# Score products of the first batch from three to two per group, with tail keys beside the local ones, and a new written order of all queues

## The chip, the cores and the metric

One core of a Trainium2 chip runs the whole kernel. The metric is the device time of one launch in microseconds (us). TensorE is called PE, VectorE DVE, ScalarE ACT, GpSimd POOL, and the queue of the sync engine, which issues nearly every DMA, SP.

## What is computed

Attention of 4 batches x 8 heads x 768 queries with head size 64, in which each query sees the keys closer than 16 to it and a summary (maximum) of every block of 32 keys; the values are v and the block means of v. The result, 3072 x 512, goes through a two-layer perceptron (512 to 2048 to 512) with GELU. All in float32 on the host side; the weights come as float64.

```python
k_sum = k.reshape(B, H, nb, block, D).max(axis=3)
v_sum = v.reshape(B, H, nb, block, D).mean(axis=3)
scores_l = scale * np.matmul(q, k.transpose(0, 1, 3, 2))
mask_l = np.abs(pos[:, None] - pos[None, :]) < window
scores_s = scale * np.einsum('bhsd,bhnd->bhsn', q, k_sum) + np.log(block)
a = softmax(np.concatenate([np.where(mask_l, scores_l, -1e9), scores_s], axis=-1))
x = np.matmul(a, np.concatenate([v, v_sum], axis=2))      # heads joined: 3072 x 512
h = x @ w_in;  g = 0.5 * h * (1.0 + erf(h * inv_sqrt2));  out = g @ w_out
```

## The kernel before

**Tiling.** Attention runs in 24 units: unit u is one batch, four heads and 256 queries, that is four query tiles of 64. Units 0 to 5 are the first batch. For a tile, 128 slots hold the keys a query may see: before the change 64 local keys in slots 0 to 63, 24 block summaries in 64 to 87 (`SLOT_SUM`), eight masked slots, and 32 tail keys in 96 to 127 (`SLOT_TAIL`). A unit has eight groups of 128 slots, four for each half of the array rows (`e`); in one group two tiles (`c`) sit in the two halves of the output partitions.

**Steps of a unit.** Units 0 to 5 are `wide`: `f_mask` (L721) lays the mask into PSUM with float16 products, and `scores_wide` (L760) adds float32 products straight from `kp0` (keys of the first batch, tail and local keys contiguous) and `ks32` (summaries). A float32 product stands as two records on PE, each with a weight load of its own. Later units split q and k into two float16 parts and multiply 48 times. Then `maximum_p` (DVE), `exponent_p` (ACT), `recip` (DVE), and a normalisation on ACT (`s_norm`) or DVE (`p_norm`). Units 0 to 2 turn the probabilities on PE (`p_turn`, kept by ACT in `p_keep`); later ones by DMA: `s_p_hi` (ACT), `p_lo` (DVE), two `turn` steps (L890, SP). `values` (L915) multiplies by v, which `load_v` brings, `s_load_vs` completes with the block means (`sum_vt`, `mean_vt`), and, from unit 3 on, `v_hi` (ACT) and `v_lo` (DVE) split. `take_hi` (ACT) and `take_lo` (DVE) take the result out of PSUM as two float16 parts of x.

**Perceptron.** Two units make one chunk of 256 tokens. `phase1h` (half of the contraction, L980) and `phase1` (L967) multiply by w_in for chunks 0 to 3, later pairs of chunks go through seven half-size `product` steps (L1004); `gelu`, `g_hi`, `g_lo` follow; `phase2` (L1073) and, for the last two pairs, `s_product`/`s_last` multiply by w_out. Weights arrive as float64 in `stage`, `gh` and `gl`, are turned to float32 by three DVE steps each (`wh_bits`, `wi_bits`, `wo_bits`) and split by `wi_hi`/`wo_hi` (ACT) and `wi_lo`/`wo_lo` (DVE). `warm` steps are products of ones whose result nobody reads.

**Order.** Nothing reorders at run time or by a planner at build time: the string `ORDER` (L74) lists 1648 steps, each is issued when its turn comes, and so every engine's queue is the sequence of its own steps in that string. The five PSUM banks (`bank`), the two `stage` halves and other rings are handed out in the same order. Around the change PE's queue begins: `warm 2`, `warm 3`, `f_mask 0`, `scores 0`, `warm 0`, `f_mask 1`, `scores 1`, `warm 1`, `f_mask 2`, `scores 2`, `p_turn 0 0`, `p_turn 0 1`, `sum_vt 0`, `p_turn 1 1`, `f_mask 3`, `scores 3`, `p_turn 1 0`, `values 0`, `sum_vt 1`, `p_turn 2 0`, `p_turn 2 1`, `f_mask 4`, `scores 4`, `values 1`, then ten `phase1h 0` steps with `values 2`, `f_mask 5`, `values 3` and `scores 5` among them, then `phase1 1 1`.

Of the kernel before, what the change touches and what calls it, by code (L numbers as in the profile page):

```python
# [1340 lines left out]
```

## Time and profile before

| what | value |
|---|---|
| median of 3 runs | 555.44 us (555.1 to 556.59) |
| the profiled execution | 556.61 us, span 554.8 us |
| PE busy | 544.9 us (98%) |
| DVE busy | 453.2 us (82%) |
| ACT busy | 425.3 us (77%) |
| DMA | 74.94 MB, mean 135 GB/s, 300 to 400 GB/s in the first 40 us |

The span runs from the first to the last instruction; the rest of the execution's time lies around it. An engine's share is a mean over stages that differ: DVE is at 82% in all, but a window of 20 us tells whether it has room there. "PEclk" is the clock that TensorE was granted, as a share of full speed. "issue" is idle time for which the profile shows no releasing event.

### The profile page before, as it was taken

How to read it: one execution, taken by the hardware profiler on the slowest of the kernel's cores; microseconds unless marked ns; L12 is line 12 of the kernel's file. 1: busy time of each engine (PE TensorE's matmuls, PEld its weight loads, DVE VectorE, ACT ScalarE, POOL GpSimd, SP SyncE). 2: the span in 40 equal slices, each digit the busy share in tenths (PEclk: the TensorE clock that was granted, in tenths of full speed). 3: DMA queues.
4: the chain of work that ended last, by engine and by line, in shares of the span. 5: the costliest groups of instructions: out<-in, count | busy, mean ns of one | idle time of the engine just before them, and what ended most of it. 6: DMA issues, size and time to landing. Idle time of an engine off the chain costs nothing.

```text
span 554.8 us, 14751 instructions
## 1 busy us (share of the span) xinstructions
PE 544.9 (98%) x6241; PEld 402.8 (73%) x6241; DVE 453.2 (82%) x638; ACT 425.3 (77%) x1005; POOL 0.8 (0%) x9
## 2 busy tenths in 40 slices
PE   8799999999999999999999999999999999999997
PEld 4678885457858665678665767756776888888886
DVE  4979999979989997989888674798799999885611
ACT  3978985759999998999999999997886585653320
POOL 0000000000000000000000000000000000000000
PEclk9989999999999999999999999999999999999999
DMA  8986585696879675554636461531440000100012
...
DMA packets 73635, 74.94 MB, mean 135 GB/s; under 512 B 46944, under 2 KB 52960, under 8 KB 73568
## 3 DMA queue, kind: packets, MB, share of 16 engines
...
q8 instruction: 49, 0.80, 0.6%
q14 instruction: 18, 0.15, 0.1%
...
## 4 chain that ended last, share of the span: by engine, by line
PE 94%; DMA 3%; DVE 1%; issue 1%; ACT 0%; SPq 0%; ACTq 0%; DVEq 0%
PE bank L1017 25%; PE bank L1080 10%; PE bank L1081 10%; PE bank L1082 10%; PE bank L1194 9%; PE ps_v L923 4%; PE bank L976 4%; PE bank L989 4%; PE bank L978 4%; PE bank L977 4%; PE ps_s L793 3%; PE ps_s L1194 2%; PE ps_v L1194 2%; PE ps_s L775 1%; DMA q<-in_qd_dram 1%; PE bank L876 1%
## 5 line engine op out<-in xcount | busy, mean ns | idle before, releaser
L1080 PE MATMUL bank<-w_out_h,gh 128*128 128x512 f16 x256 | 97.1, 379 | 0.0
L1081 PE MATMUL bank<-w_out_l,gh 128*128 128x512 f16 x256 | 97.0, 379 | 0.0
L1082 PE MATMUL bank<-w_out_h,gl 128*128 128x512 f16 x256 | 97.0, 379 | 0.0
L1017 PEld LDWEIGHTS <-w 128*128 128x128 f16 x640 | 62.0, 98 | 9.3
L1017 PEld LDWEIGHTS <-w_in 128*128 128x128 f16 x576 | 55.9, 98 | 8.6
L833 ACT ACTIVATE s<-s,s_top 128x128 f32<-128x128 f32 x144 | 55.8, 394 | 0.1
L1067 DVE SCALAR_TENSOR_TENSOR gl<-g,gh 128x512 f16<-128x512 f32 x76 | 51.0, 683 | 4.0 <-ACT gh L1063 3.9
L1063 ACT ACTIVATE gh<-g 128x512 f16<-128x512 f32 x76 | 46.6, 626 | 3.4 <-PE bank L1081 2.8
L1082 PEld LDWEIGHTS <-gl 128*128 128x128 f16 x256 | 25.1, 98 | 30.2
L1017 PE MATMUL bank<-x,w_in 128*128 128x256 f16 x384 | 46.6, 273 | 0.0
L1029 DVE TENSOR_TENSOR g<-bank,late 128x512 f32<-128x512 f32 x48 | 32.9, 686 | 14.3 <-PE bank L1017 13.8
L1080 PEld LDWEIGHTS <-gh 128*128 128x128 f16 x256 | 25.0, 98 | 26.7
L1081 PEld LDWEIGHTS <-gh 128*128 128x128 f16 x256 | 25.1, 98 | 26.0
L1017 PE MATMUL bank<-stage,w 128*128 128x256 f16 x320 | 44.0, 273 | 0.0
L1023 ACT ACTIVATE late<-bank 128x512 f32<-128x512 f32 x48 | 28.0, 591 | 20.6 <-PE bank L1017 19.9
L1017 PE MATMUL bank<-x,w 128*128 128x256 f16 x320 | 43.6, 273 | 0.0
L978 PE MATMUL bank<-x,w_in 128*128 128x256 f16 x144 | 39.3, 273 | 0.0
L976 PE MATMUL bank<-x,w_in 128*128 128x256 f16 x144 | 39.3, 273 | 0.0
L977 PE MATMUL bank<-x,w_in 128*128 128x256 f16 x144 | 39.2, 273 | 0.0
L1049 ACT ACTIVATE g<-bank 128x512 f32<-128x512 f32 x48 | 28.0, 589 | 9.2 <-PE bank L978 4.8
L1049 ACT ACTIVATE g<-g 128x512 f32<-128x512 f32 x48 | 29.2, 624 | 5.3 <-DVE g L1029 5.0
L870 ACT ACTIVATE s<-s,s_rec 128x128 f32<-128x128 f32 x104 | 31.8, 391 | 0.4 <-DVE s_rec L848 0.4
...
## 6 DMA issues: line engine op xcount, KB each, us to landing
...
```

The source lines that it names most:

```text
L833: nc.scalar.activation(self.s32[:, gs], score[:, ss], AF.Exp, bias=self.top[:, g : g + 1], scale=scale, accum_out=self.den[:, g : g + 1],)
L976: nc.tensor.matmul(dst, wh, xh, start=(k == 0), stop=False)
L977: nc.tensor.matmul(dst, wh, xl, start=False, stop=False)
L978: nc.tensor.matmul(dst, wl, xh, start=False, stop=(k == NCC - 1))
L1017: nc.tensor.matmul(dst, l, r[:, k], start=(first and e == 0 and k == 0 and n == 0), stop=(k == KH - 1 and n == 2), skip_group_check=True,)
L1049: nc.scalar.activation(g, h, AF.Gelu, scale=1.0 / (SC_X * SC_WI))
L1063: nc.scalar.activation(gh, two(g_slot(c, i)), AF.Copy, scale=SC_G)
L1067: nc.vector.scalar_tensor_tensor(out=gl, in0=two(g_slot(c, i)), scalar=SC_G, in1=gh, op0=ALU.mult, op1=ALU.subtract)
L1080: nc.tensor.matmul(t, gh[:, f, js], w_out_h[:, f, :], start=(n == 0), stop=False)
L1081: nc.tensor.matmul(t, gh[:, f, js], w_out_l[:, f, :], start=False, stop=False)
L1082: nc.tensor.matmul(t, gl[:, f, js], w_out_h[:, f, :], start=False, stop=(n == NFC - 1))
L1194: nc.tensor.matmul(acc[:, t * NH : (t + 1) * NH], a[:, f, js], b[:, f], start=(first and j == 0 and t == 0 and f == 0 and n == 0), stop=(f ...
```

## The change

Two things change together. First, for batch 0 the slots are laid out as 64 local keys, 32 tail keys, 24 summaries, eight masked ones. Local and tail keys are contiguous in `kp0`, so `scores_wide` makes one product of 96 columns and one of 24 for each tile instead of three of 64, 24 and 32: 32 float32 products per unit instead of 48, over the same 120 columns. The mask, the summary rows of `sum_vt`, `mean_vt`, `load_vs`, and the host layout of v follow; the number and size of their instructions stay, but for the 96 + 24 instead of 64 + 24 output rows of `sum_vt`. Second, `ORDER` is replaced: it holds the same 1648 steps with the same arguments in another sequence, on all queues. Of the order the part up to about 80 us is shown, old and new.

```diff
@@ -27,6 +27,7 @@
 KW = TQ + BLOCK
 SLOT_SUM = TQ
 SLOT_TAIL = TQ + BLOCK
+WIDE_TAIL, WIDE_SUM = TQ, TQ + BLOCK
@@ ORDER @@
-fetch_k 0 0, load_m16, load_q 0, fetch_k 0 1, fetch_wh 1 1, load_q 1, fetch_w_in 4, warm 2 9, warm 3 3, f_mask 0,
-prep_k 0 0, scores 0, maximum_p 0, prep_k 0 1, warm 0 12, f_mask 1, scores 1, exponent_p 0, fetch_wh 6 1, load_eye,
-load_q 2, warm 1 1, f_mask 2, scores 2, fetch_vt 0, fetch_wh 1 0, load_ind, load_q 3, fetch_wh 6 0, fetch_vt 1,
-load_v 0, fetch_w_in 2, wh_bits 1 1 0, wh_bits 1 1 1, wh_bits 1 1 2, recip 0, wi_hi 1 1, s_norm 0, fetch_w_in 0,
-load_v 1, load_q 4, p_turn 0 0, p_turn 0 1, sum_vt 0, wi_bits 4 0, maximum_p 1, wi_bits 4 1, exponent_p 1,
-wi_lo 1 1, wi_bits 4 2, maximum_p 2, wh_bits 6 1 0, wi_hi 4 1, exponent_p 2, wi_hi 4 0, p_keep 0 1, mean_vt 0,
-recip 1, wh_bits 1 0 0, p_norm 1, wh_bits 6 1 1, wh_bits 1 0 1, wh_bits 6 1 2, wi_lo 4 1, wh_bits 6 0 0,
-wh_bits 1 0 2, recip 2, wi_lo 4 0, wh_bits 6 0 1, p_keep 0 0, s_load_vs 0, p_turn 1 1, f_mask 3, scores 3,
-p_turn 1 0, values 0, fetch_wh 7 1, load_v 2, s_norm 2, maximum_p 3, wi_bits 2 0, take_hi 0, sum_vt 1, p_turn 2 0,
-p_turn 2 1, exponent_p 3, p_keep 1 1, mean_vt 1, p_keep 1 0, wh_bits 6 0 2, wi_bits 2 1, take_lo 0, f_mask 4,
-scores 4, s_load_vs 1, values 1, phase1h 0 4 0, wi_bits 0 0, wi_bits 2 2, wi_bits 0 1, wi_hi 1 0, recip 3,
-wi_bits 0 2, wi_hi 6 0, wi_hi 2 0, wi_hi 0 0, p_keep 2 1, take_hi 1, s_load_vs 2, p_keep 2 0, wi_hi 6 1,
-wh_bits 7 1 0, wi_lo 1 0, p_norm 3, wi_lo 6 0, wi_lo 0 0, take_lo 1, maximum_p 4, phase1h 0 1 0, phase1h 0 6 0,
-s_p_hi 3, wi_hi 2 1, exponent_p 4, values 2, wi_hi 0 1, take_hi 2, fetch_w_out 4, fetch_wh 7 0, fetch_w_in 3,
-load_v 3, load_q 5, turn 3 0, s_load_vs 3, v_hi 3, wi_lo 6 1, wi_lo 2 0, wh_bits 7 0 0, wh_bits 7 1 1, wo_bits 4 0,
-p_lo 3, wh_bits 7 0 1, turn 3 1, wh_bits 7 1 2, wh_bits 7 0 2, wi_lo 2 1, wi_lo 0 1, take_lo 2, v_lo 3, wi_bits 3 0,
-wo_bits 4 1, recip 4, wo_bits 4 2, phase1h 0 0 0, phase1h 0 6 1, phase1h 0 4 1, f_mask 5, phase1h 0 1 1,
-phase1h 0 2 0, phase1h 0 2 1, values 3, gelu 0 4, gelu 0 1, take_hi 3, g_hi 0 4, g_hi 0 1, take_lo 3, fetch_w_in 5,
-phase1h 0 0 1, scores 5, load_v 4, s_norm 4, wo_hi 4, wi_hi 7 0, s_load_vs 4, gelu 0 0, g_hi 0 0, gelu 0 2,
-wi_bits 3 1, wi_bits 5 0, g_lo 0 1, g_lo 0 4, wi_bits 5 1, wo_lo 4, phase1 1 1, phase1 1 4, phase1 1 6,
-fetch_w_out 0, wi_bits 5 2, wo_bits 0 0, wi_bits 3 2, wi_hi 5 1, v_hi 4, wi_lo 5 1, wo_bits 0 1, wi_hi 3 0,
-wi_hi 5 0, gelu 0 6, gelu 1 1, g_hi 0 6, wi_lo 5 0, wo_bits 0 2, wi_lo 7 0, v_lo 4, fetch_w_out 1, wo_hi 0,
-g_hi 1 1, g_lo 1 1, g_lo 0 0, wo_lo 0, phase1 1 2, gelu 1 4, g_hi 1 4, phase1 1 0, phase1h 0 5 0, phase1h 0 5 1,
-phase1 1 5, wi_hi 7 1, s_p_hi 4, wi_hi 3 1, fetch_w_out 7, load_q 7, load_v 5, wi_lo 3 0, gelu 1 0, g_hi 0 2,
-gelu 0 5, wo_bits 1 0, g_lo 1 4, wo_bits 1 1, wi_lo 3 1, wo_bits 1 2, gelu 1 5, wo_hi 1, g_hi 1 0, wi_lo 7 1,
...
+fetch_k 0 0, load_m16, load_q 0, fetch_k 0 1, load_eye, load_q 1, fetch_wh 6 1, fetch_wh 1 1, warm 2 9, warm 3 3,
+f_mask 0, prep_k 0 0, scores 0, maximum_p 0, prep_k 0 1, warm 0 12, f_mask 1, scores 1, load_q 2, fetch_wh 6 0,
+fetch_wh 1 0, fetch_vt 0, load_ind, fetch_w_in 4, load_q 3, load_v 0, fetch_vt 1, fetch_w_in 0, wh_bits 6 1 0,
+wh_bits 6 1 1, wh_bits 6 1 2, exponent_p 0, wi_hi 6 1, fetch_w_in 2, load_v 1, recip 0, s_norm 0, wh_bits 1 1 0,
+wh_bits 1 1 1, wh_bits 6 0 0, wh_bits 1 1 2, maximum_p 1, wh_bits 6 0 1, wi_hi 1 1, exponent_p 1, wi_lo 1 1,
+wh_bits 6 0 2, wh_bits 1 0 0, warm 1 1, f_mask 2, scores 2, maximum_p 2, p_turn 0 1, p_turn 0 0, sum_vt 0,
+wi_hi 6 0, exponent_p 2, p_keep 0 1, mean_vt 0, p_keep 0 0, s_load_vs 0, recip 1, wh_bits 1 0 1, p_norm 1,
+wi_lo 6 0, wi_bits 4 0, wh_bits 1 0 2, wi_hi 1 0, wi_lo 6 1, wi_bits 4 1, recip 2, wi_bits 4 2, s_norm 2,
+p_turn 1 0, p_turn 1 1, f_mask 3, scores 3, values 0, p_keep 1 1, p_keep 1 0, take_hi 0, maximum_p 3, wi_lo 1 0,
+sum_vt 1, p_turn 2 1, p_turn 2 0, mean_vt 1, exponent_p 3, s_load_vs 1, wi_bits 0 0, wi_bits 0 1, take_lo 0,
+wi_bits 0 2, phase1h 0 6 0, phase1h 0 1 0, f_mask 4, values 1, wi_bits 2 0, wi_bits 2 1, load_q 4, fetch_wh 7 1,
+recip 3, wi_hi 4 1, wi_hi 4 0, wi_hi 0 0, wi_bits 2 2, wi_hi 2 0, take_hi 1, wh_bits 7 1 0, scores 4, load_q 5,
+load_v 2, fetch_wh 7 0, fetch_w_in 3, fetch_w_out 4, p_keep 2 1, p_keep 2 0, s_load_vs 2, wi_hi 2 1, wi_lo 4 0,
+wh_bits 7 1 1, take_lo 1, phase1h 0 4 0, wi_lo 4 1, wi_lo 2 0, p_norm 3, phase1h 0 6 1, values 2, load_v 3,
+s_p_hi 3, turn 3 0, wi_lo 0 0, maximum_p 4, wi_lo 2 1, wh_bits 7 0 0, wi_bits 3 0, wh_bits 7 0 1, p_lo 3, take_hi 2,
+wi_hi 0 1, wi_lo 0 1, wh_bits 7 0 2, wh_bits 7 1 2, turn 3 1, exponent_p 4, wo_bits 4 0, take_lo 2, s_load_vs 3,
+v_hi 3, v_lo 3, phase1h 0 4 1, phase1h 0 2 0, phase1h 0 2 1, phase1h 0 0 0, phase1h 0 1 1, f_mask 5, scores 5,
+values 3, phase1h 0 0 1, wo_bits 4 1, gelu 0 6, wi_hi 7 1, wi_lo 7 1, wi_hi 7 0, take_hi 3, take_lo 3, wo_bits 4 2,
+wi_bits 3 1, gelu 0 0, gelu 0 4, wo_hi 4, recip 4, fetch_w_in 5, fetch_kx 3 3, load_q 6, fetch_w_out 0, load_v 4,
+wi_bits 5 0, wi_bits 3 2, wi_bits 5 1, wo_lo 4, s_norm 4, g_hi 0 0, s_p_hi 4, gelu 0 1, g_hi 0 4, g_hi 0 1,
+g_lo 0 0, wi_bits 5 2, wi_hi 5 1, wi_hi 3 1, gelu 0 2, wo_bits 0 0, g_lo 0 4, wi_lo 7 0, wo_bits 0 1, wi_lo 5 1,
+fetch_w_out 1, wo_bits 0 2, phase1 1 1, phase1 1 6, phase1 1 0, phase1 1 4, gelu 1 0, gelu 1 4, g_hi 1 0,
+s_load_vs 4, wi_hi 5 0, g_lo 1 0, p_lo 4, wi_lo 5 0, wo_hi 0, gelu 1 1, v_hi 4, wo_lo 0, v_lo 4, wi_hi 3 0,
+wo_bits 1 0, g_hi 1 1, g_hi 1 4, g_lo 0 1, wi_lo 3 1, g_lo 1 4, wo_bits 1 1, wi_lo 3 0, g_hi 0 2, wo_bits 1 2,
+phase1 1 7, phase1h 0 7 0, phase1h 0 7 1, phase1 1 5, phase1h 0 5 0, turn 4 0, turn 4 1, gelu 1 7, gelu 1 5,
+g_hi 0 6, wo_hi 1, load_v 5, s_load_vs 5, g_hi 1 5, load_q 7, fetch_w_out 7, load_mask, fetch_w_out 5, maximum_p 5,
+wo_lo 1, g_lo 0 6, wo_bits 7 0, g_lo 1 1, wo_bits 7 1, wo_bits 7 2, values 4, phase1 1 2, phase1h 0 3 0,
...
@@ -594,12 +595,12 @@
         total = bank.use(f"vt{h}", 2)
         for j in range(NTT):
             nc.tensor.matmul(
-                total[: SLOT_SUM + NBLK, :VH], ind_sb[:, P - SLOT_SUM + j * NBLK : P + (j + 1) * NBLK], vt0[:, h, j],
+                total[: WIDE_SUM + NBLK, :VH], ind_sb[:, P - WIDE_SUM + j * NBLK : P + (j + 1) * NBLK], vt0[:, h, j],
                 start=(j == 0), stop=(j == NTT - 1),
             )
 
     def mean_vt(h):
-        rows = slice(SLOT_SUM, SLOT_SUM + NBLK)
+        rows = slice(WIDE_SUM, WIDE_SUM + NBLK)
         nc.scalar.activation(
             vm0[rows, h * VH : (h + 1) * VH], bank.use(f"vt{h}", 2)[rows, :VH], AF.Copy, scale=1.0 / BLOCK
         )
@@ -690,7 +691,7 @@
 
         def load_vs(self, scalar=False):
             if self.b == 0:
-                rows = slice(SLOT_SUM, SLOT_SUM + NBLK)
+                rows = slice(WIDE_SUM, WIDE_SUM + NBLK)
                 means = vm0[rows, self.h0 * D : (self.h0 + UH) * D].rearrange("p (r e d) -> p r e d", r=NR, d=D)
                 means = means.unsqueeze(1).broadcast_to([NBLK, CT, NR, 2, D])
                 dst = self.v32[rows].rearrange("p (t r e) d -> p t r e d", t=CT, e=2)
@@ -733,7 +734,7 @@
                     cs = slice(c * TQ, (c + 1) * TQ)
                     dst = pse[e][cs].rearrange("p (n j) -> p n j", j=P)
                     nc.tensor.matmul(
-                        dst[:, :, SLOT_SUM : SLOT_SUM + NBLK], two[:, cs],
+                        dst[:, :, WIDE_SUM : WIDE_SUM + NBLK], two[:, cs],
                         logb.unsqueeze(1).broadcast_to([2, NG // 2, NBLK]), start=False, stop=False, skip_group_check=True,
                     )
 
@@ -762,20 +763,19 @@
             pse = [self.ps(e) for e in range(2)]
             for g in range(NG // 2):
                 r, t2 = g // 2, g % 2
-                for part in range(3):
+                for part in range(2):
                     for e in range(2):
                         for c in range(2):
                             rows, t = slice(e * D, (e + 1) * D), 2 * t2 + c
                             at, kb = g * P, c0 + t * TQ
                             at, k = (
-                                (at, kp0[rows, r0 + r, kb : kb + TQ]),
-                                (at + SLOT_SUM, ks32[rows, r0 + r]),
-                                (at + SLOT_TAIL, kp0[rows, r0 + r, kb + TQ : kb + TQ + P - SLOT_TAIL]),
+                                (at, kp0[rows, r0 + r, kb : kb + WIDE_SUM]),
+                                (at + WIDE_SUM, ks32[rows, r0 + r]),
                             )[part]
                             nc.tensor.matmul(
                                 pse[e][c * TQ : (c + 1) * TQ, at : at + k.shape[1]],
                                 self.q32[rows, (r * CT + t) * TQ : (r * CT + t + 1) * TQ], k,
-                                start=False, stop=(g == NG // 2 - 1 and part == 2),
+                                start=False, stop=(g == NG // 2 - 1 and part == 1),
                             )
 
         def scores(self):
@@ -1262,7 +1262,8 @@
 
 
 def _mask16():
-    m = _mask()[:, : (CT + 2) * TQ]
+    m = _mask()[:, : (CT + 2) * TQ].reshape(P, -1, P)
+    m = np.concatenate([m[:, :, :SLOT_SUM], m[:, :, SLOT_TAIL:], m[:, :, SLOT_SUM:SLOT_TAIL]], axis=2).reshape(P, -1)
     two, logb = np.zeros((P, P)), np.zeros((P, NBLK))
     two[:2] = 1.0
     logb[0] = np.float16(LOGB)
@@ -1289,7 +1290,8 @@
         for t in range(CT):
             r = (t0 + t) * TQ
             vw[u, :TQ, t] = vp[b, r : r + TQ, hs]
-            vw[u, SLOT_TAIL:, t] = vp[b, r + TQ : r + TQ + BLOCK, hs]
+            tail = SLOT_TAIL if b else WIDE_TAIL
+            vw[u, tail : tail + BLOCK, t] = vp[b, r + TQ : r + TQ + BLOCK, hs]
     qd, kd, vw = (a.reshape(nu, a.shape[1], -1) for a in (qd, kd, vw))
     kp = np.ascontiguousarray(k.transpose(0, 1, 3, 2).reshape(B, H // 2, P, S))
     kp[B - 1] = kp[B - 1].transpose(1, 0, 2).reshape(H // 2, P, S)
```

## Rows read from the trace of the kernel before

**Rows 1.** The profile page: span, and busy time, share and instructions by engine.
```profile
span 554.8 us, 14751 instructions
PE 544.9 (98%) x6241; PEld 402.8 (73%) x6241; DVE 453.2 (82%) x638; ACT 425.3 (77%) x1005; POOL 0.8 (0%) x9
```

**Rows 2.** Windows: length, busy PE, PEld, DVE, ACT, POOL; PEclk, DMA share, GB/s.
```profile
20.00:40.00 20.00, 17.48 (x319) 14.40 (x321) 17.11 (x32) 15.79 (x53) 0.00 (x0) 0.91 0.94 364
40.00:60.00 20.00, 19.96 (x339) 16.74 (x333) 19.83 (x30) 18.30 (x44) 0.00 (x0) 1.00 0.73 228
...
340.00:360.00 20.00, 19.55 (x236) 15.02 (x235) 14.42 (x21) 19.97 (x42) 0.00 (x0) 1.00 0.45 99
```

**Rows 3.** Chain of work that ended last, by time: start us, us, what.
```profile
17.98 1.65 PE bank L876 x13
19.62 0.72 issue
20.34 0.60 PE bank L876 x3
20.95 2.59 PE bank L596 x12
23.54 0.89 PE bank L876 x8
24.43 0.55 PE ps_s L730 x4
24.98 0.20 PE ps_s L735 x4
25.18 1.53 PE ps_s L775 x96
26.71 2.18 issue
28.89 1.67 PE bank L876 x8
...
58.31 0.22 PE bank L976
...
71.73 2.62 PE bank L989 x24
...
347.33 6.28 DMA pt<-p_l
```

**Rows 4.** DMA queues of the page: packets, MB, share of 16 engines.
```profile
q8 instruction: 49, 0.80, 0.6%
```

**Rows 5.** Timeline of PE in `scores 3`: start us, us, line, tile, shape, count.
```profile
25.27 0.26 PE L775 MATMUL ps_s<-misc,q 64*64 64x24 f32 x8
25.36 0.44 PE L775 MATMUL ps_s<-w_out_l,q 64*64 64x32 f32 x16
25.62 0.26 PE L775 MATMUL ps_s<-misc,q 64*64 64x24 f32 x8
```

**Rows 6.** Timeline of DVE from 10 to 36 us: `prep_k 0 1`, then pairs of neighbours.
```profile
10.02 1.75 DVE L555 TENSOR_REDUCE misc<-w_out_l 128x48 f32<-128x1536 f32 x1
...
23.17 0.68 DVE L406 SCALAR_TENSOR_TENSOR w<-gl,w 128x512 int32<-128x512 int32 x1
23.77 0.68 DVE L410 SCALAR_TENSOR_TENSOR w<-stage,w 128x512 int32<-128x512 int32 x1
...
34.35 1.22 DVE L410 SCALAR_TENSOR_TENSOR w<-gh,w 128x1024 int32<-128x1024 int32 x1
35.48 1.22 DVE L406 SCALAR_TENSOR_TENSOR w<-gh,w 128x1024 int32<-128x1024 int32 x1
```

**Rows 7.** Timeline of SP: the second `turn` of unit 3.
```profile
48.56 1.31 SPq L892 DMA_TRANSPOSE pt<-p_l  x1
```

**Rows 8.** Timeline of PE: after the stall in `scores 1`; and `values 3`.
```profile
14.29 0.18 PE L775 MATMUL bank<-misc,q 64*64 64x24 f32 x1 [0.94 <-issue]
...
54.42 0.95 PE L923 MATMUL ps_v<-pt,v_hl 128*64 128x64 f16 x48
```

More of the change, by code (lines that the diff above doesn't have):

```diff
@@ L115 @@
-g_hi 2 1, gelu 2 0, p_lo 6, load_q 10, load_k 10, turn 6 1, put 0 1, scores 8, phase1 2 2, phase1 2 6, t_add 1 0,
-recip 7, prep_k 2 0, v_hi 6, s_q_hi 9, gelu 2 4, gelu 2 2, g_hi 2 4, g_hi 2 0, s_k_hi 9, g_hi 2 2, v_lo 6, g_lo 2 1,
-load_v 7, fetch_v 3 0, values 6, phase1 2 3, add_mask 8, q_lo 9, p_norm 7, k_lo 9, gelu 2 6, g_hi 2 6, store 1 0,
-s_q_hi 10, take_hi 6, s_p_hi 7, s_k_hi 10, g_lo 2 0, q_lo 10, maximum 8, g_lo 2 6, take_lo 6, scores 9, phase1 2 5,
-phase1 2 7, phase2 1 7, k_lo 10, p_lo 7, g_lo 2 4, add_mask 9, exponent 8, recip 8, t_add 1 1, load_vs 7, load_k 11,
@@ L120 @@
-turn 7 1, turn 7 0, load_k 12, load_q 11, gelu 2 5, g_hi 2 5, v_hi 7, prep_v 3 0, prep_k_end 2 0, v_lo 7, load_v 8,
-fetch_k 2 1, put 1 0, load_vs 8, load_q 12, gelu 2 3, g_hi 2 3, store 1 1, s_norm 8, gelu 2 7, g_hi 2 7, phase2 2 0,
-phase2 2 1, values 7, t_add 1 2, t_add 1 3, g_lo 2 5, t_add 0 0, phase2 2 4, maximum 9, take_hi 7, s_p_hi 8,
-s_k_hi 11, s_q_hi 11, take_lo 7, g_lo 2 2, t_add 0 1, k_lo 11, t_add 2 1, q_lo 11, phase1 3 1, phase1 3 0,
-exponent 9, v_hi 8, prep_k 2 1, p_lo 8, turn 8 0, g_lo 2 3, recip 9, prep_k_end 2 1, p_norm 9, scores 10,
@@ new lines @@
+k_lo 8, maximum 7, exponent 7, phase1 2 0, phase1 2 4, scores 8, phase1 2 5, phase2 1 7, load_k 9, load_q 10,
+gelu 2 4, gelu 2 0, gelu 2 5, g_hi 2 5, s_q_hi 10, s_k_hi 9, g_hi 2 4, fetch_k 2 0, turn 6 0, prep_v 1 1, load_vs 6,
+put 0 1, load_q 11, load_k 10, p_lo 6, add_mask 8, recip 7, t_add 1 0, maximum 8, prep_k 2 0, t_add 0 1, phase1 2 1,
+phase1 2 3, v_hi 6, store 1 1, gelu 2 1, s_k_hi 10, gelu 2 3, g_hi 2 1, k_lo 9, scores 9, s_q_hi 11, turn 6 1,
+v_lo 6, p_norm 7, g_lo 2 5, prep_k_end 2 0, g_lo 2 1, values 6, g_hi 2 0, take_hi 6, s_p_hi 7, g_hi 2 3, exponent 8,
@@ new lines @@
+fetch_v 3 0, load_v 7, fetch_v 3 1, load_k 11, put 1 1, load_vs 7, turn 7 0, phase1 2 7, phase1 2 6, gelu 2 6,
+g_lo 2 0, take_lo 6, phase2 2 1, phase1 2 2, prep_v 3 0, q_lo 10, g_lo 2 3, phase2 2 0, t_add 1 1, p_lo 7,
+add_mask 9, g_lo 2 4, turn 7 1, k_lo 10, t_add 2 1, recip 8, s_k_hi 11, v_hi 7, v_lo 7, k_lo 11, gelu 2 7,
+store 1 0, s_norm 8, values 7, take_hi 7, scores 10, gelu 2 2, s_p_hi 8, phase2 2 5, take_lo 7, maximum 9,
+load_q 12, load_v 8, put 0 0, prep_v 3 1, q_lo 11, t_add 1 2, p_lo 8, exponent 9, s_q_hi 12, q_lo 12, recip 9,
@@ new lines @@
+v_lo 10, product 2 0 1, phase2 3 1, values 10, scores 13, s_q_hi 14, t_hi 0 0, s_p_hi 11, p_lo 11, t_hi 0 1,
+g_hi 3 6, gelu 3 7, maximum 12, exponent 12, keep 2 0 0, sx_hi 2 1, t_lo 0 0, product 2 1 1, phase2 2 7, g_lo 3 5,
+phase2 3 0, phase2 3 3, load_v 11, turn 11 0, load_vs 11, store 2 1, v_hi 11, g_hi 3 7, t_lo 0 1, t_hi 1 0,
+x_take 10, turn 11 1, load_q 15, g_lo 3 4, add_mask 13, phase2 3 5, t_add 3 0, put 2 0, k_lo 14, load_k 16, q_lo 14,
+maximum 13, sx_lo 2 1, product 2 0 2, exponent 13, v_lo 11, g_lo 3 7, t_add 3 1, values 11, scores 14, g_lo 3 6,
```

267 lines of the change are left out of this document (130 added, 137 removed).

## The prediction

> **What bounds the kernel now.** I read the page first: PE is busy for 544.9 of 554.8 us [rows 1], so no edit on another engine helps unless PE idles for it, and only 9.9 us of idle time exist. The windows then say where: PE idles 2.52 us between 20 and 40, 0.04 between 40 and 60 and 0.45 between 340 and 360 [rows 2]; the other windows up to 540 are full, and what remains lies in the first 20 us and behind the last product. So PE is the bound from about 29 us to the end, and its start is the only place with something to win. There the chain names two stalls that wait for nothing the profile shows, 0.72 us inside `p_turn 0` and 2.18 us after `scores 3` [rows 3]; a third, 0.94 us, stands in `scores 1` [rows 8]. DVE is the second engine to look at: it is busy for 19.83 of 20 us between 40 and 60 and idles only 2.89 between 20 and 40 [rows 2]. Whoever starts PE earlier must ask whether DVE can follow.
>
> **The stalls.** Between the second and the third stall PE takes 3 + 12 + 8 + 4 + 4 + 96 = 127 records [rows 3], each with its weight load: 254 instructions, 256 with two waits. The page counts 2 x 6241 PE instructions [rows 1], and one instruction queue moved 49 packets, 0.80 MB in all [rows 4]: 16 KB and about 255 instructions each. So PE's instructions come in pages of 256, and each of these stalls is a late page. One page is asked for, I take it, when the one before is entered: the page entered at 20.34 was followed by one at 28.89, 8.55 us later, and the one entered at 14.29 by the one at 20.34, 6.05 us later [rows 3, 8]. The Trainium skill, "Runtime: NRT & Kernel Launch", section "Instruction fetch mechanics", gives the same 256 instructions in 16 KiB blocks, fetched while the current block runs, and calls the crossing mostly hidden. By that rule these stalls would be nothing; the trace disagrees with its 0.94, 0.72 and 2.18 us while the DMA share is 0.94.
>
> **Part 1, the products.** A float32 product of 24 columns and its three partners occupy 25.27 to 25.36, 0.09 us; one of 32 and one of 64 together 0.26 [rows 5]; four such groups make the 1.53 us of a unit [rows 3]. The new product of 96 columns has no row. I bound it by the 0.26 of the two that it replaces and by the 0.16 that is left for 64 columns if 32 take 0.10, a little more than 24. A straight line through 32 and 64 columns gives 0.22; the floor is a cost per instruction alone. I take 0.20, nearer to the line: 0.06 saved in a group, 0.24 in a unit, with bounds of 0 and 0.4. Six units: 1.4 us (0 to 2.4). In units 0 to 2 PE waits anyway, so 0.7 of it is on the path. The 64 instructions fewer per unit count more: a page then lasts longer while the transfers are dense. The mask, `sum_vt`, `mean_vt` and `load_vs` keep number and size of their instructions; I cost them at nothing.
>
> **Part 2, the order at the start.** Counted from the front, the page borders before lie at instructions 188, 444 and 700. In the new queue 188 falls into `warm 0`, at about 10.4 us (an estimate: `scores 0` ends 0.24 earlier, ten products follow), 444 into `scores 2` (record 45 of 64), 700 into `scores 3` (record 57 of 64). With 6.05 to 8.55 us per page they open at 16.4 to 19.0 and 22.5 to 27.5.
> DVE decides how much of that is felt, because in the new order PE has nothing in reserve behind it. I add up DVE's queue from `prep_k 0 1`, which starts at 10.02 now [rows 6] and 0.2 earlier after the shorter `scores 0`. Start to start, a step over 512 columns takes 0.60 us and one over 1024 takes 1.13 [rows 6]. Up to `wi_lo 5 0`, which `phase1 1 5` reads, the new queue has 76 steps: 40 x 0.60 = 24.0, 20 x 1.13 = 22.7, and 16 others (maxima, reciprocals, half-size bit steps, the key maximum) about 11.0, in all 57.7. Without any idle time it ends at 9.8 + 57.7 = 67.5. In it `maximum_p 2` stands at 18.8 and `maximum_p 3` at 27.3, so the two late pages cost DVE nothing at the early ends and 0.5 us at the late ones.
> Idle time to add: about 0.9 us in all for `recip 1`, `take_lo 0` and `take_lo 1`, which in ACT's queue stand behind `exponent_p 1`, two `p_keep` and four `wi_hi`; and a wait of `take_lo 3` for `values 3`. `values 3` needs the second `turn` of unit 3, which SP issues when `p_lo 3` is done, at 45.6 + 0.9 = 46.5. Two rows price that DMA: 6.28 us at 347 [rows 3], where PE waited for it, and at most 5.9 in unit 3, from 48.56 to 54.42 [rows 7, 8], where nothing shows that it was awaited. I take 5.4 (4.5 to 6.3): `values 3` runs at 52.0 to 52.9, `take_hi 3` on ACT to 53.5, and `take_lo 3`, free on DVE at 52.4, waits 1.2 us. All steps behind it on DVE wait too, weight steps first, then `g_lo`. So `wi_lo 5 0` ends at 67.5 + 0.9 + 1.2 = 69.6, and PE begins `phase1 1 5` at about 69.8. PE by its own queue: 52.9, `phase1h 0 0 1` 1.31 (24 products take 2.62 [rows 3]), then 144 products of the same kind, 15.7: 69.9. The two agree.
> Before, PE has done the same ten halves and `scores 5` at 58.31 [rows 3], and with the same 15.7 would stand there at 74.0. The gain at this point is 74.0 - 69.9 = 4.1 us, of which part 1 is 0.7.
>
> **Part 2, the rest.** `values 4` moves from behind seven `phase2` steps to the place behind `phase1 1 5` and `phase1h 0 5 0`. Its second `turn` follows `p_lo 4`, on DVE at 66.9 + 2.1 = 69.0; with 5.4 us it lands at 74.4, while PE arrives at 69.9 + 2.62 + 1.31 = 73.8: 0.6 lost (0 to 1.5), with `phase1 1 2` and all behind it. After that DVE's sum leaves PE some 3 us or more in reserve at every `g_lo`, `wo_lo`, `k_lo` and `v_lo` up to 150 us; later reserves I can't read from sums and take as before, where one stall of 0.45 in 480 us is all [rows 2]: 0.2 more lost. On SP, the loads that wait for a buffer (`load_v 3` for `values 2`, `fetch_w_out 1` for `wi_bits 5 2`) stand ahead of the turns but are free before them. The end keeps its form: `s_last`, one `s_end`, one store. Sum: 4.1 - 0.6 - 0.2 = **3.3 us less**. The profiled execution has 1.8 us around its span and lies 1.2 above the median of the runs; I take the gain from the median: 555.4 - 3.3 = **552.1 us**.
>
> **The rivals.** A, no idle on DVE: the turns land in 4.5 us and ACT keeps up. Then `wi_lo 5 0` ends at 67.5 and the gain is up to 6.3: 549.1. For it: the DVE rows show no idle inside dense stretches. Against: the 0.9 on ACT is queued work.
> B, the late pages come back: what the fetch costs depends on the DMA traffic, and a page of 8.55 us followed by another opens 700 at 27.5, where `maximum_p 3`, `values 0`, `take_hi 0` and `p_turn 2` are next. After the 2.18 us stall the granted clock fell to 0.91 on average in that window [rows 2] (eight turning products took 1.67 us instead of 0.89 [rows 3]): 1.8 us of full speed lost, the clock standing at 1.2 of 2.4 GHz for a part of it. One such loss and 0.5 late: 555.4 - 3.3 + 2.3 = 554.4. By the rule of the Trainium skill named above no page would be late at all: this case would fall away and the forecast stay.
> C, slower: DVE idles more than it can afford. Each us of idle on DVE between 10 and 67 goes to PE at `phase1 1 7` and `phase1 1 5`, where the new order leaves 0.2 us. It decides from 74.0 - 0.2 - 67.5 = 6.3 us of idle. Before it was 3.1 in 20 to 60 us [rows 2], with PE's stalls as cause; ACT, on which DVE's `g_lo`, `v_lo` and `wo_lo` wait, gets the same work in less time. With 8.5 us: 557.6.
> D, the products gain nothing and neither does the order (DVE idles as much as PE gains): 555.2.
>
> **Chances.** Forecast 0.50 (550.2 to 553.7), A 0.15, B 0.15, C 0.13, D 0.07. A measurement of this kernel can tell 0.3%, 1.7 us, from no change: faster than 553.8 is the forecast and A, 0.65; B and D within it, 0.22; C slower, 0.13. The range 549.0 to 556.6 leaves out the best part of A and most of C.
>
> **What would show it.** Right: the stalls without releaser at the page borders stand in `scores 2` and `scores 3`, the one of 2.18 us is gone, `values 0` begins at about 26 us (now it comes after the stall that ends at 28.89 [rows 3]), `phase1 1 1` at 54 to 55, and a unit's scores at 1.2 to 1.4 us. `take_lo 3` waits for `take_hi 3`. Wrong: `phase1 1 5` later than 72; PE idle between 76 and 540 of over 2 us in sum; a granted clock under 0.9 in a second window; scores of a unit at 1.53 still (part 1 nothing) or near 1.0 (cost per instruction).

## The result and the profile after

The changed kernel takes 549.92 us (549.75 to 549.95) where the kernel before took 555.58 in the same comparison: the ratio is 0.9895, with a 95% interval of 0.9878 to 0.9912. That is 5.7 us less; 3.3 were forecast. The profiled execution of before lay 1.2 us above the median of its runs, the one of after has a span of 548.1, so the two traces differ by 6.7 us, and it is the traces that the rest of this section compares. Lines of after, and of the experiments, can stand one or a few higher than those of before.

The page, the windows and the list of what PE waited for (line, releaser, us in total, times, longest) of the kernel after:

```profile
span 548.1 us, 14376 instructions
PE 539.9 (98%) x6049; PEld 401.0 (73%) x6049; DVE 452.8 (83%) x638; ACT 429.7 (78%) x1009; POOL 0.8 (0%) x9
...
0.00:20.00 20.00, 16.55 (x260) 10.36 (x261) 12.41 (x21) 10.12 (x41) 0.76 (x9) 1.00 0.93 354
20.00:40.00 20.00, 18.89 (x299) 15.99 (x298) 19.76 (x32) 19.70 (x64) 0.00 (x0) 1.00 1.04 405
40.00:60.00 20.00, 20.00 (x299) 17.36 (x298) 19.73 (x28) 17.66 (x42) 0.00 (x0) 1.00 0.72 216
...
PE bank L597 <- ACT s L833: 1.8, 1, 1.8
PE bank L876 <- DVE s L865: 1.1, 1, 1.1
PE bank L965 <- POOL ones L382: 0.9, 1, 0.9
PE ps_s L775 <- DMA q<-in_qd_dram: 0.3, 1, 0.3
PE ps_s L775 <- DVE misc L556: 0.2, 1, 0.2
```

PE is still the bound, with the same share of a shorter span. No wait without a releaser ("issue") is left; before there were three [rows 3, 8]. Between 20 and 40 us the granted clock is 1.00, where it was 0.91 [rows 2], and DVE, which idled there, is busy for 19.76 of 20 us. All of PE's remaining waits lie ahead of 23.4 us; from there to the last product PE is never idle, and the stall of 0.45 us at 353 [rows 2] is gone. The timeline of PE shows the new start (start, duration, the wait in brackets):

```profile
14.09 0.40 PE L775 MATMUL ps_s<-w_out_l,q 64*64 64x96 f32 x8 [0.33 <-DMA q<-in_qd_dram]
14.39 0.38 PE L775 MATMUL ps_s<-w_out_l,q 64*64 64x96 f32 x8
14.59 0.26 PE L775 MATMUL ps_s<-misc,q 64*64 64x24 f32 x8
...
15.34 2.25 PE L876 MATMUL bank<-misc,s 128*128 128x128 f32 x16
19.43 2.85 PE L597 MATMUL bank<-w_out_h 128*120 128x256 f32 x12 [1.84 <-ACT s L833]
23.40 2.02 PE L876 MATMUL bank<-misc,s 128*128 128x128 f32 x16 [1.11 <-DVE s L865]
...
27.36 1.15 PE L923 MATMUL ps_v<-pt,v 128*64 128x64 f32 x32
...
51.18 0.95 PE L923 MATMUL ps_v<-pt,v_hl 128*64 128x64 f16 x48
...
53.38 0.27 PE L976 MATMUL bank<-x,w_in 128*128 128x256 f16 x1
...
69.10 0.27 PE L976 MATMUL bank<-x,late 128*128 128x256 f16 x1
...
73.12 0.95 PE L923 MATMUL ps_v<-pt,v_hl 128*64 128x64 f16 x48
```

`scores 2` runs from 14.09 to 15.34: 1.25 us for a unit, where a unit took 1.53 [rows 3]. `values 0` starts at 27.36, `values 3` at 51.18, `phase1 1 1` at 53.38 (58.25 before), `phase1 1 5` at 69.10, `values 4` at 73.12, each without a wait.

**Where the 6.7 us are.** Adding up PE's steps from start to start in both traces: the front part (`warm`, `f_mask`, `scores` of units 0 to 5, `p_turn`, `sum_vt`, `values` of units 0 to 2) takes 42.9 us before and 38.2 after, 4.7 less. Of these, 1.2 are idle time (4.8 before, 3.6 after), 1.7 are the products (6 x 0.28), and the remaining 1.8 are full speed: before, the trace has PE at 1.2 instead of 2.4 GHz from 29.4 to 32.8 us, behind its stall of 2.18 us [rows 2, 3]. All other steps together take 507.26 us before and 505.34 after, 1.92 less, and that was not forecast. Here 29 steps of the perceptron no longer have a `values`, `scores` or `f_mask` step right behind them, and together they are 2.70 us shorter; 19 others now have one, and are 1.72 longer; `values 19` is 0.62 shorter, of which 0.45 is its stall; 0.3 remain. (That stall is not shown to be the order's: two experiments below that keep the old order, part 1 alone and the borders moved in the kernel before, run `values 19` without it too.) This is an accounting, not yet a cause; the causes are what the experiments are for.

### The profile page after: what moved, and what is told of

The parts are those of the page before. It is cut to its first block, busy times and chain, and to the rows that moved or that the text cites. A ratio compares the mean times of both kernels' runs of the same rounds, so it can differ in the third digit from the quotient of the medians.

```text
span 548.1 us, 14376 instructions
## 1 busy us (share of the span) xinstructions
PE 539.9 (98%) x6049; PEld 401.0 (73%) x6049; DVE 452.8 (83%) x638; ACT 429.7 (78%) x1009; POOL 0.8 (0%) x9
## 4 chain that ended last, share of the span: by engine, by line
PE 95%; DMA 2%; DVE 2%; issue 0%; ACT 0%; SPq 0%; ACTq 0%
PE bank L1017 27%; PE bank L1080 10%; PE bank L1081 10%; PE bank L1082 10%; PE bank L1194 10%; PE ps_v L923 4%; PE bank L976 4%; PE bank L989 4%; PE bank L977 4%; PE bank L978 4%; PE ps_s L793 3%; PE ps_s L1194 2%; PE ps_v L1194 2%; DMA stage<-in_w_in_dram 1%; PE ps_s L775 1%; DMA w_out_l<-in_kp_first_dram 1%
## 5 line engine op out<-in xcount | busy, mean ns | idle before, releaser
L1049 ACT ACTIVATE g<-g 128x512 f32<-128x512 f32 x48 | 29.4, 624 | 9.1 <-DVE g L1029 9.0
```

Source lines behind the costliest of these rows:

```text
L1049: nc.scalar.activation(g, h, AF.Gelu, scale=1.0 / (SC_X * SC_WI))
```

## The experiments

My theory for the start was: PE's instructions come in pages of 256, a stall without a releaser is a late page, and DVE's queue sets how early PE can follow. A border is the place in PE's queue at which one page ends and the next begins. The rivals were that the two parts simply add up (products by their own time, order by its own), and that PE's own waits or the transfers set the start. For the body the question was what one neighbour of another kind costs.

### Part 1 alone

```diff
-ORDER = (the new order)
+ORDER = (the order of before; 32 products and the new slots stay)
```

> The old order with the 32 products of the new slot layout (part 1 alone). Page theory (PE's instructions come in pages of 256, and a stall without a releaser is a late page): 32 records fewer in each of scores 0, 1 and 2 move the borders, from scores 1 to scores 2 (record 46 of 64) and from scores 3 to p_turn 1 0 (record 2 of 8); at both places PE comes later than the pages land, so the stalls of 0.94, 0.72 and 2.18 us shrink to under 0.5 each, the clock's fall after the last goes with them, and the time is 551.5 us (550.5 to 553.5). Rival, the products only save their own time: 0.28 us in each of the units where PE doesn't wait, the stalls stay at 2 us or more in sum somewhere in the first 30 us: 554.6 (554.0 to 555.2).

It takes 551.66 us (551.39 to 551.86; ratio 0.9900, 0.9875 to 0.9924), where the kernel before took 556.66 on the same chip (555.40 to 558.34). Two of PE's waits in the first 40 us, from its timeline, and the second window:

```profile
16.62 0.40 PE L776 MATMUL ps_s<-w_out_l,q 64*64 64x96 f32 x8 [2.86 <-DMA q<-in_qd_dram]
20.26 2.82 PE L598 MATMUL bank<-w_out_h 128*120 128x256 f32 x12 [0.34 <-DMA w_out_h<-in_mask_dram]
...
20.00:40.00 20.00, 19.37 (x297) 16.36 (x298) 19.83 (x35) 18.98 (x59) 0.00 (x0) 1.00 1.02 396
```

No wait without a releaser is left, in the old order, though not one step was moved, and the clock stays at 1.00. The products alone bring 5.0 us by the medians, three times their own 1.7. PE now waits 2.86 us for q of unit 2, which lands at 16.6, and still `phase1 1 1` starts at 53.9, 4.4 us earlier than before. The theory of pages holds here, and the rival (554.6) falls. Added up step by step as above, the front part takes 42.9 us before, 38.6 here and 38.2 in the kernel after: with 32 products the new order adds 0.4 us there and 1.1 in the body, 1.5 in all.

### Part 2 alone

```diff
-for part in range(2): ... kb : kb + WIDE_SUM (96 columns), then 24
+for part in range(3): ... kb : kb + TQ (64), then 24, then kb + TQ : kb + WIDE_SUM (32)
```

> The new order, but 48 products per unit (the 96 columns in two products of 64 and 32). Page theory: the borders lie where they lay in number, which is now scores 1 record 86, p_turn 0 1 record 13 of its two steps, scores 3 record 89 of 96; a stall of 0.5 to 1 us in scores 1, one of up to 3 us in p_turn that is hidden by the wait of p_turn 1 for DVE at 23.3 us, and 0 to 2 us in scores 3. With 0.28 us more for each of units 3, 4 and 5: 551.3 us (550.6 to 553.5). Rival, the order alone does everything and the pages never matter in it: no stall without releaser, 550.8 or less.

It takes 558.78 us (556.95 to 560.24), a ratio of 1.0039 (1.0019 to 1.0059): with 48 products the new order is slower than the kernel before, and 7.5 us above the 551.3 expected. The profiled execution is the fastest of the ten, 556.95. The waits without releaser from PE's timeline, and two windows:

```profile
13.81 0.18 PE L776 MATMUL bank<-misc,q 64*64 64x24 f32 x1 [0.48 <-issue]
19.86 0.60 PE L877 MATMUL bank<-misc,s 128*128 128x128 f32 x3 [1.55 <-issue]
...
29.38 0.18 PE L776 MATMUL ps_s<-misc,q 64*64 64x24 f32 x1 [1.92 <-issue]
...
58.82 0.27 PE L978 MATMUL bank<-x,w_in 128*128 128x256 f16 x1 [2.33 <-issue]
...
40.00:60.00 20.00, 17.67 (x385) 15.12 (x374) 18.90 (x28) 17.13 (x39) 0.00 (x0) 0.98 0.64 181
60.00:80.00 20.00, 20.00 (x173) 17.26 (x171) 16.64 (x21) 14.46 (x26) 0.00 (x0) 0.93 0.52 161
```

The first three stalls are where they were expected. The fourth, 2.33 us in `phase1 1 1`, was not: it stands at record 986 of PE's queue, 764 behind the first, which is six pages of 127 or 128. Behind it the granted clock falls to a mean of 0.93, and the step in which it stands is 1.83 us longer than in the kernel after beyond the stall itself. What went on when that page was wanted is seen in the transfers (GB/s in forty slices of the stretch, then the queues), first for 53 to 56.5 us, then for 56.5 to 57.75, and last the loads that SP issued from 50.8 to 51.8 us:

```profile
GB/s 304 164 164 187 211 187 281 445 304 281 304 304 374 398 421 398 398 374 538 421 374 421 374 374 398 445 375 375 445 468 445 375 398 398 375 398 398 398 398 398
...
GB/s 590 721 525 262 197 328 197 197 262 131 131 66 0 131 0 0 0 0 0 0 0 0 0 0 0 0 0 0 0 0 0 66 0 0 0 0 0 0 66 0
...
q8 instruction: 1, 0.02, 4.7%
...
stage<-in_w_in_dram SPq DMA_DIRECT2D x1, 1024.0 KB
ot<-in_kp_dram SPq DMA_DIRECT2D x1, 256.0 KB
q<-in_qd_dram SPq DMA_DIRECT2D x1, 256.0 KB
```

The page border before lies at 53.0, inside `scores 5`. From about 54 to 56.6 us these loads run at about 400 GB/s and no page moves; when they end the one page comes (its packet runs from 56.56 to 57.50), and PE goes on at 58.82. Meanwhile the 128 records of the page before were used up in 3.6 us, because `scores 5` and `values 3` stand side by side in the new order and have short records. So the order and the products are not two gains that add up: alone they give -5.0 and +2.1 us against the kernel before on their chip, together -5.7 in the comparison above.

### The borders moved in the kernel before

```diff
-        for _ in range(n):                          # warm 0: 12 products of 512 columns
+        for _ in range(2 * n if k == 0 else n):     # 24 of 256
...
```

> The kernel before with the twelve 512-column products of warm 0 made as 24 of 256 columns: the same columns, 12 more records, result unused in both. Page theory: the three stalls without releaser stand 12 records earlier in the queue: record 74 of scores 1 instead of 86, the first records of p_turn 0 0 instead of the thirteenth or so, record 84 of 96 in scores 3 instead of just behind it, and again 127 or 128 records apart. Rival, a stall belongs to its step (a late operand, a queue): it stays behind scores 3 and in the same place of p_turn 0.

```profile
13.65 0.28 PE L775 MATMUL bank<-w_out_l,q 64*64 64x64 f32 x3 [0.41 <-issue]
16.38 0.34 PE L775 MATMUL ps_s<-w_out_l,q 64*64 64x64 f32 x8 [1.21 <-DMA q<-in_qd_dram]
19.70 1.94 PE L876 MATMUL bank<-misc,s 128*128 128x128 f32 x15 [1.41 <-issue]
28.86 0.24 PE L775 MATMUL ps_s<-misc,q 64*64 64x24 f32 x2 [1.59 <-issue]
```

All three stalls stand 12 records earlier in the code: the third, behind `scores 3` before [rows 3], is now inside it, with 12 of its 96 records to go, and the second comes behind one record of `p_turn 0 0`. Counted in PE's queue they are at records 222, 350 and 477 in both kernels (a fourth, of 0.15 us, stands at record 987, in `scores 5`). A stall that belonged to its step would have stayed. The trace shows the pages themselves: in the six kernels that have such stalls there are 18 of them, and each ends 1.3 to 1.6 us after a packet of 16 KB in the instruction queue has ended (in the kernel before, packets end at 12.95, 18.82 and 27.26, and PE goes on at 14.29, 20.34 and 28.89). The time, 554.99 us in one execution, is below the median of before on that chip, 556.66, and within its range; behind a stall of 1.59 us instead of 2.18 the clock stayed at 1.00.

### The borders moved in the kernel after

Two kernels make `warm 0` into more, shorter products, 78 and 59 records more.

```diff
-        for _ in range(n):                                                  # 12 x 512 columns
+        for w in n * [DM] if k else 88 * [D] + 2 * [DM // 2]:               # 78 more
+        for w in n * [DM] if k else 64 * [D] + 4 * [DM // 4] + 3 * [DM]:    # 59 more
...
```

> The kernel after with the twelve 512-column products of warm 0 made as 90 products (88 of 64 columns, two of 256): the same columns, 78 more records, result unused in both. Page theory: every border lies 78 records earlier in the queue. One then falls to the front of scores 5, so that the next 128 records (scores 5, values 3 and what follows) are used up in 3.9 us, while a page came 5.8 us after the border before in the run that changed the order alone: a stall without releaser of about 2 us near 51 us, and one of about 0.5 in scores 1. PE is the bound behind 23 us, so the 2 us count: 551.9 (551.0 to 554.0, the upper end if the clock falls behind the stall). Rival, in the new order the place of the borders doesn't matter: no stall, 549.9.

> The kernel after with the twelve products of warm 0 made as 71 (64 of 64 columns, 4 of 128, 3 of 512): the same columns, 59 more records, result unused in both. Every border lies 59 records earlier; one falls to record 4 of the 64 of scores 5. The run with 78 records had it 15 slow product records before scores 5, and its page was already on the way. Theory (a page is asked for when PE's queue, which runs some records ahead of the array, comes to the border before; among the short records of scores and values that lead is worth little time): from here the next 128 records take 4.3 us against 5.8 from border to border in the run that changed the order alone: a stall without releaser of 1 to 1.5 us in phase1 1 1, time 551.2 (550.6 to 553.0). Rival (the place of a border is of no account once the first 30 us are over): no stall, 550.1 (549.9 to 550.3).

They take 550.17 us (550.00 to 550.68) and 549.90 (549.79 to 550.21): within 0.3 us of after. The first stall comes back in both, in `scores 1` (0.75 in the first, 0.59 here), the one near 51 us doesn't. In the first, a page is late once more far behind the start: `scores 7`, at 125 us, waits at record 1498 of PE's queue, ten pages behind 222, and takes 0.41 us longer than in the kernel after. The row of that wait from the first, then PE's timeline of the second and the transfers of its stretch from 47 to 50 us:

```profile
PE ps_s L793 <- issue: 0.2, 1, 0.2
...
13.72 0.30 PE L775 MATMUL bank<-misc,q 64*64 64x24 f32 x5 [0.59 <-issue]
...
GB/s 34 0 0 0 0 0 0 0 0 0 7 126 246 276 297 294 283 297 287 287 294 294 280 182 263 4 0 0 0 0 0 0 27 27 191 82 164 219 273 246
...
q8 instruction: 1, 0.02, 2.1%
```

Both expectations of a stall of 1 to 2 us failed, and with them the idea that the place of a border decides. In the second the transfers rest at 48.8 to 49.3 us, the page in question moves from 48.82 to 49.85, just before PE enters the page ahead of it, and so it is there in time although the 128 records of that one are used up in 4.2 us. In the kernel after, a page moves only at 54.37, 3.3 us after PE entered the page ahead of it, with loads at 376 GB/s in between, and no stall follows: the 128 records last 9.4 us. Together with part 2 alone: a border costs when its page is wanted during loads at about 400 GB/s and short records follow; neither is enough alone. No run here moves a load while the border stays, so of the two conditions the first rests on these traces and not on a test.

### The border moved in the new order with 48 products

```diff
     nc.tensor.matmul(dst, eye_[:, cs], self.masks(mask16_sb, NR), start=True, stop=False)
+    m, pj = self.masks(mask16_sb, NR), (2 * P if self.edge else P) // 32
+    for j in range(15 if self.u == 4 else 0):        # f_mask 4: 60 records more
+        part = m[:, j // pj, j % pj * 32 : j % pj * 32 + 32]
+        nc.tensor.matmul(dst[:, j * 32 : j * 32 + 32], eye_[:, cs], part, start=False, stop=False)
```

> The new order with 48 products, and in f_mask 4 sixty more products of 32 columns that add the mask once more to masked slots, so that the mask is doubled there and the probabilities stay 0. Behind f_mask 4 every border lies 60 records earlier: the one in record 31 of scores 5 goes to phase1h 0 0 0. Page theory: the stall of 2.33 us in phase1 1 1 and the fall of the clock behind it (1.8 us) go, the sixty products cost about 1 us: 555.0 to 556.5 where the run without them gave 558.8. Rival (that loss belongs to the order, with 48 products, and not to the border): 559 to 560.

It takes 557.02 us (554.69 to 558.74; ratio 1.0012, 0.9993 to 1.0031), 0.5 above the upper end of what was expected. The stall in `phase1 1 1` is gone, and the windows of the profiled execution (555.68) show the clock:

```profile
40.00:60.00 20.00, 19.52 (x440) 16.98 (x436) 16.40 (x24) 14.93 (x34) 0.00 (x0) 1.00 0.63 160
60.00:80.00 20.00, 20.00 (x224) 17.80 (x223) 19.96 (x26) 17.56 (x33) 0.00 (x0) 1.00 0.60 193
```

Step by step against part 2 alone, `phase1 1 1` is 4.16 us shorter, the 2.33 of the stall and the 1.83 of lost speed; `f_mask 4` is 2.01 longer, twice what I had allowed for its sixty products; and `scores 4` 0.70, 0.47 of it a new late page. So the loss at 58 us belongs to the border and not to the order. The third stall, 1.92 us in `scores 3`, is still there. In the profiled execution the clock stayed at 1.00 behind it; eight of the other nine had a mean granted clock of 0.992 to 0.997 and took 556.7 to 558.7 us; where it fell in those is not on record.

### Values and scores side by side

A first try moved eleven `scores` steps behind the next step of PE's queue:

```diff
-... values 7, scores 10, gelu 2 2, s_p_hi 8, phase2 2 5, ...
+... values 7, gelu 2 2, s_p_hi 8, phase2 2 5, scores 10, ...
```

> The kernel after with eleven scores steps of units 6 to 23, which stand right beside a values step, moved behind the next product step of PE's queue. Theory (each change from a step that uses the full array to one that uses half of it costs about 0.09 us more on PE, and the new order has 23 such changes where the old had 32): 11 x 0.09 = 1.0 us more than after, 550.9 (550.5 to 551.5), without new waits on PE. Rival, the gain of the body comes from elsewhere: within 0.3 us of after, 549.9.

In the written order some of them then stand behind the steps that read their scores, so these units compute with other scores. It took 556.80 us (555.17 to 558.79), with two new waits of 2.0 us on PE for `ps_s`, at 241.8 and 323.5 us, and tells nothing on the question. The second try leaves all readers in place and pulls one product step between the two, at thirteen places:

```diff
-... values 10, scores 13, s_q_hi 14, ... t_lo 0 0, product 2 1 1, ...
+... values 10, product 2 1 1, scores 13, s_q_hi 14, ... t_lo 0 0, ...
```

> The kernel after with one product step pulled between the scores step and the values step at thirteen places where the two stand side by side (units 6 to 23); all steps stay. Theory (each change from a step that uses the full array to one that uses half of it costs about 0.09 us more on PE; the new order has 23 such changes, the old 32): 13 x 0.09 = 1.2 us more than after, 551.1 (550.7 to 551.7), without new waits on PE. Rival, the body's gain comes from elsewhere: within 0.3 us of after, 549.9.

It takes 554.84 us (554.24 to 555.64; ratio 0.9980, 0.9967 to 0.9994), against 549.98 (549.80 to 550.24) for the kernel after on the same chip. PE's timeline of one place, first of the kernel after on this chip, then of this kernel:

```profile
200.92 1.48 PE L1017 MATMUL bank<-x,w_in 128*128 128x256 f16 x12
202.24 0.38 PE L1080 MATMUL bank<-w_out_h,gh 128*128 128x512 f16 x1
```

```profile
203.27 1.48 PE L1018 MATMUL bank<-x,w_in 128*128 128x256 f16 x12
204.68 0.25 PE L794 MATMUL ps_s<-kk,qh 64*64 64x128 f16 x4
```

The same `product 2 1 1` occupies PE for 1.32 us where a full-array step follows (200.92 to 202.24) and for 1.41 where a half-array step does (203.27 to 204.68): 0.09 us. It is 0.09 at every one of the thirteen places in the trace, 1.2 in sum, as expected. The time rose by 4.9 and not by 1.2 because five other steps of PE became longer by 0.2 to 0.8 us each, 3.2 in sum. PE's new waits there are for ACT and DVE, which may be the units that were held up by one step; this was not tested:

```profile
PE bank L1081 <- ACT g L1050: 0.6, 1, 0.6
PE bank L977 <- ACT g L1050: 0.6, 1, 0.6
PE bank L1081 <- ACT ot L1087: 0.6, 1, 0.6
PE ps_s L794 <- DVE kk L755: 0.4, 1, 0.4
```

The size of the switch is settled; that the order has so little slack that one step of 1.3 or 2.6 us costs three times the switches was not expected.

### What sets the start

```diff
-wh_bits 1 1 1, wh_bits 6 0 0, wh_bits 1 1 2, maximum_p 1, ...
+wh_bits 1 1 1, wh_bits 1 1 2, maximum_p 1, wh_bits 6 0 0, ...
```

The kernel after, unchanged, ran beside it:

> The kernel after once more, unchanged, so that the small differences of the runs beside it are taken on the same chip: 549.9 us (549.6 to 550.2).

> The kernel after with wh_bits 6 0 0 moved behind maximum_p 1 on DVE: the maximum of unit 1 then fills the 0.86 us in which DVE waits at 14.5 to 15.3 us for a half of stage. Theory (DVE's sum sets the start, PE follows it from p_turn 1 at 23.4 us on): p_turn 1 begins 0.8 us earlier and the time falls by 0.6 to 0.9: 549.2. Rival (PE's own queue or the transfers set the start): under 0.2 less, 549.8.

After takes 549.98 us (549.80 to 550.24), this 549.71 (549.21 to 549.87). DVE's wait of the kernel after is gone, PE starts `p_turn 1 0` at 22.82 instead of 23.28 (23.40 above), and the 0.47 us stay with every step of PE up to a new wait at 90.8; behind it 0.08 are left. A row of DVE in after, then two of PE here:

```profile
15.35 0.43 DVE L402 TENSOR_SCALAR w<-stage 128x512 int32<-128x512 int32 x1 [0.86 <-DMA stage<-in_w_in_dram]
```

```profile
22.82 0.46 PE L877 MATMUL bank<-misc,s 128*128 128x128 f32 x2 [1.08 <-DVE s L866]
...
90.77 0.38 PE L1081 MATMUL bank<-w_out_h,gh 128*128 128x512 f16 x1 [0.23 <-ACT g L1050]
```

The start moved as the theory says, but the time did not fall by the 0.6 to 0.9 us expected: the medians differ by 0.27, and their ranges overlap. DVE got 0.6 of its 0.86 us, PE 0.47 of them, and 0.39 went again at 90.8 (0.23 of them stand as a wait), where ACT waits for DVE and DVE, 0.95 us at 79.9, for a half of `stage` from w_out. A second edit brings that load forward:

```diff
-... load_v 5, s_load_vs 5, g_hi 1 5, load_q 7, fetch_w_out 7, load_mask, ...
+... fetch_w_out 7, load_v 5, s_load_vs 5, g_hi 1 5, load_q 7, load_mask, ...
```

> The kernel after with wh_bits 6 0 0 behind maximum_p 1, as before, and besides fetch_w_out 7 ahead of load_v 5 and load_q 7 on SP. In the first of the two edits alone every PE step from p_turn 1 to 90 us stood 0.47 us earlier, and then PE waited 0.23 for a chain that begins with DVE waiting 0.95 us at 79.9 for a half of stage from w_out. Theory: the earlier load lets the gain stand: 0.45 less than after, 549.5 (549.3 to 549.7). Rival: load_v 5 and load_q 7 come later and what waits for them takes it back: 549.7 to 550.0.

549.54 us (549.36 to 549.75; ratio 0.9879, 0.9859 to 0.9899), while the kernel with 59 records more, which does nothing else, took 549.90 on the same chip. In the trace the 0.47 us stay to the end: the last product ends at 543.84 instead of 544.31. It is the fastest version here, 0.4 us below the kernel after, and shows that from 23 us on a step gained at the start is kept if nothing that DVE or ACT waits for lands later.

The opposite edit was meant to take away the longest wait of PE itself, and leaves DVE alone:

```diff
-... exponent_p 1, wi_lo 1 1, wh_bits 6 0 2, wh_bits 1 0 0, warm 1 1, f_mask 2, ...
+... warm 1 1, exponent_p 1, wi_lo 1 1, wh_bits 6 0 2, wh_bits 1 0 0, f_mask 2, ...
```

> The kernel after with warm 1 ahead of exponent_p 1 in the written order: every engine's queue stays, but sum_vt 0 gets the bank that warm 1 leaves and not one of scores 1, so its wait of 1.8 us for exponent_p 1 goes. Theory (DVE sets the start): p_turn 1 waits for p_norm 1 until 23.3 as before, 1.8 us longer, and the time stays at 549.9 (549.7 to 550.2; up to 551.7 if the longer idle time makes the clock fall). Rival (PE's own waits set the start): 548.1.

```profile
18.99 2.82 PE L598 MATMUL bank<-w_out_h 128*120 128x256 f32 x12 [1.29 <-DMA w_out_h<-in_mask_dram]
23.44 2.02 PE L877 MATMUL bank<-misc,s 128*128 128x128 f32 x16 [1.62 <-DVE s L866]
```

550.47 us in one execution, above the 549.7 to 550.2 expected; 0.39 us of it is `values 5` at 117 us, which now waits for a `turn`. Of the wait of 1.84 us only a part went: `sum_vt 0` starts at 18.99 instead of 19.43, now held by a load, and `p_turn 1 0` waits 1.62 instead of 1.11 us for `p_norm 1` and starts at 23.44, not earlier than before. So the 0.44 us that PE gained were worth nothing: the start is DVE's, and the rival's 548.1 falls.

## Why the prediction was right, and where it was off

**The direction and the bound.** Right: PE bounds from the start of `p_turn 1`, its start is the place with something to win, and DVE decides when it comes; the last three experiments show it from both sides. But DVE holds PE only at `p_turn 1 0` (1.11 us) and nowhere behind it. The prediction let DVE decide at `phase1 1 5`, 46 us later, and there PE did not wait.

**Part 1.** A unit's scores take 1.25 us; 1.2 to 1.4 was named. The saving is 0.28 a unit where 0.24 was taken, and a group of 96 columns 0.20 (14.39 to 14.59), as taken. That the 64 instructions fewer count more than the columns was right in kind and left out of the sum, and this is its largest error: part 1 alone brings 5.0 us, where the sum had 0.7 and put the other 2.6 under the order, which alone costs 2.1. That in units 0 to 2 PE waits anyway was no reason to count nothing there: what it waited for were in part the late pages, and these went with the records.

**The late pages.** Wrong: they were forecast in `scores 2` and `scores 3`, and no stall without releaser is in the trace. The failed step is the price: 6.05 to 8.55 us from one border to the next was read as what a page takes from the entry of the one before. It is not a constant. The first page can be used at 13.6 to 14.3 us in all six kernels whose border lies in `scores 1`, at whatever record. In the traces a page's packet starts up to 7.1 us after PE has entered the page before when loads of about 400 GB/s run, and at 42 to 46 us, where they rest in six of the kernels, between 1.0 us ahead of that and 1.1 us behind. The step changed no number, because the sum had DVE hide both pages. Of the rule of the Trainium skill, "Runtime: NRT & Kernel Launch", section "Instruction fetch mechanics" (256 instructions to a block, the crossing mostly hidden): the first half agrees with borders at 222, 350 and 477; the second holds for the kernel after and fails with 2.33 us in part 2 alone.

**DVE's sum.** `phase1 1 5` was forecast at 69.8 to 69.9 and starts at 69.10; `values 3` at 52.0, and starts at 51.18. `wi_lo 5 0`, which should have ended at 69.6, ends at 68.80, 0.3 us ahead of PE. The 57.7 us of work held (58.1 between 9.61 and 68.80); the idle term was 2.1 and measures 1.1 (0.86 for `stage`, 0.20 at `take_lo 3`). It was the wrong wait, too: not ACT's queue but the order of the loads. `values 3` follows `scores 5` without a wait, so the turn's 5.4 us, one of the two uncertain terms, was not on the path, and stays unmeasured.

**The rest.** Wrong in size and sign: 0.6 us for `values 4` and 0.2 for later steps were to be lost. `values 4` starts at 73.12 without a wait (73.8 was forecast for PE's arrival), and the body gains 1.9. The missing term is the neighbour of a step, 0.09 us for each product step ahead of `values` or `scores`: it could have been read before, since `values` and `scores` are listed with 128*64 and 64*64 and the step ahead of them is longer.

**The sum.** 3.3 forecast; 0.8 more because DVE's queue ended earlier, 0.6 and 0.2 not lost, 1.9 gained in the body: 6.8, against 6.7 between the traces. The profiled execution of before was 1.2 above its median and that of after was not, which leaves 5.6 of the 5.7 measured. The chances had 549.9 in rival A (no DVE idle, 549.1), and half of that is what happened; the other half no rival had. The direction was reasoned, the size in part luck: 0.7 and 2.6 were forecast for the two parts, and neither is near what the part does alone (-5.0 and +2.1).
